# Linear attention plus a gated product on one core: softmax sums carried in the state matrix, one key pass instead of two, and work moved between engines

## Chip, cores, metric

One core of one Trainium2 chip. The metric is device time in microseconds (us) of one execution, as the median of several.

## The reference, cut to what matters

```python
xn = _layernorm(x)                                   # x: 2048 x 512, bf16
# branch A: linear attention, 32 heads of 16
q, k, v = split(xn @ wqkv)                           # per head
pq, pk  = q @ w_phi, k @ w_phi                       # per head, 16 x 16
phi_q   = concat(softmax(pq), softmax(-pq))          # 32 features
phi_k   = concat(softmax(pk), softmax(-pk))
kv, z   = phi_k^T @ v, sum_s phi_k
o       = (phi_q @ kv) / (phi_q . z + 1e-6)
A       = o.reshape(S, D) @ wo
# branch B: gated product
B       = ((xn @ w_gate) * (xn @ w_up)) @ w_down     # F = 1792
return x + A + B
```

## The kernel before

`w_phi` is folded into the q and k weights at the start (transposes and `fold`), so that one product gives `pk` or `pq`. Then come three stages: the key side (layer norm, exp, softmax, `kv`), the query side, and a closing stage with the output products. The gated branch (called GLU below: `gps`, `ups`, `g_sb`, `hT_all`) depends on the layer norm alone. The scheduler, which fixes the order of instructions when the program is built, uses its matmuls to fill TensorE (PE) in the first two stages. Cuts are marked `...`.

```python
def ln_group(ng):                      # 4 tiles of 128 tokens
    ...
    nc.scalar.activation(out=rstd[:], in_=mv[:, 1:2], func=AF.Sqrt, bias=eps_t[:], scale=1.0)
    nc.vector.reciprocal(out=rstd[:], in_=rstd[:])
    ...                                # xn, four transposes for each of 4 column groups
    nc.vector.tensor_copy(out=xnT[...], in_=tp[:])

def a1_tile(p, n, kvps):               # key side; runs for p = 0, 1 and 16 tiles: half the heads each
    pkps = ...                         # 4 matmuls of 512 columns: 256 of pk, 256 of v
    nc.scalar.activation(out=e2k[:, 0, :], in_=pkps[:, 0:2 * P], func=AF.Exp, scale=1.0)
    nc.scalar.activation(out=e2k[:, 1, :], in_=pkps[:, 0:2 * P], func=AF.Exp, scale=-1.0)
    nc.vector.tensor_reduce(out=sums[:], ...); nc.vector.reciprocal(out=rs..., in_=sums[:])
    nc.vector.tensor_tensor(out=phik..., in0=e2k..., in1=rs..., op=ALU.mult)      # 512 wide
    nc.scalar.copy(out=vt[:, :, :, 0:DH], in_=pkps[:, 2 * P:4 * P]...)
    ...                                # 4 matmuls of 136 columns into kvps

# query side, per 256 tokens (m), half (hf) and column group (cql):
    pq = ...                           # 4 matmuls of 256 columns
    nc.scalar.activation(out=ep[:], in_=pq[:], func=AF.Exp, scale=1.0)
    nc.scalar.activation(out=em[:], in_=pq[:], func=AF.Exp, scale=-1.0)
    nc.tensor.matmul(swp[:], lhsT=BO16f, rhs=em[:], start=True, stop=True)   # softmax sums
    nc.tensor.matmul(swm[:], lhsT=BO16f, rhs=ep[:], start=True, stop=True)
    nc.vector.tensor_tensor(out=phip[:], in0=ep[:], in1=swp[:], op=ALU.mult)
    nc.vector.tensor_tensor(out=phim[:], in0=em[:], in1=swm[:], op=ALU.mult)
    for t4 in range(2):                # 256 columns, of which 8 heads x 32
        nc.tensor.matmul(nds[t4][...], lhsT=phip[:, t4 * P:(t4 + 1) * P], rhs=KVZ[:, cq, 0, :], start=True, stop=False)
        nc.tensor.matmul(nds[t4][...], lhsT=phim[:, t4 * P:(t4 + 1) * P], rhs=KVZ[:, cq, 1, :], start=False, stop=True)
    ...                                # on DVE: two small steps, reciprocal, product, copy of oT

# closing stage, per 512 tokens: 14 GLU steps (4 gps + 4 ups matmuls of 512 columns), then
    ...                                # fin: 14 + 4 matmuls of 512 columns, add x, store
```

The sums are used crosswise (`ep` is multiplied by the sum over `em`), because the common factor cancels in the division at the end.

The softmax here doesn't subtract the row's maximum and nothing guards it: scores larger than these inputs give would overflow.

## Time and profile before

| | before |
|---|---|
| median | 271.49 us (271.35 to 272.33, 4 runs) |
| span of the profiled run | 269.6 us |
| granted clock | 1.00 |
| matmuls | 1504, of 566,272 columns |

In the profile, PE is TensorE, PEld its weight loads, DVE VectorE, ACT ScalarE, POOL GpSimd and SP the engine that issues loads and stores. The cuts are the first `kv` product (28.05 us), the end of the last one (104.02) and the first `fin` matmul (173.58). Columns: the stretch, its length, then busy time of PE, PEld, DVE, ACT and POOL, clock, DMA share, GB/s.

```profile
0.00:28.05 28.05, 17.51 (x106) 8.94 (x108) 17.64 (x56) 12.92 (x28) 6.08 (x24) 1.00 0.99 330
28.05:104.02 75.97, 73.74 (x468) 37.35 (x477) 70.47 (x158) 51.67 (x137) 5.04 (x29) 1.00 0.02 7
104.02:173.58 69.56, 68.78 (x493) 44.84 (x498) 61.06 (x219) 29.44 (x75) 0.00 (x0) 1.00 0.00 1
173.58:269.60 96.02, 92.16 (x416) 40.93 (x422) 25.04 (x43) 9.38 (x16) 0.00 (x0) 1.00 0.07 23
```

DVE is 93% busy on the key side (70.47/75.97) and 88% on the query side.

### The profile page before, as it was taken

How to read it: one execution, taken by the hardware profiler on the slowest of the kernel's cores; microseconds unless marked ns; L12 is line 12 of the kernel's file. 1: busy time of each engine (PE TensorE's matmuls, PEld its weight loads, DVE VectorE, ACT ScalarE, POOL GpSimd, SP SyncE). 2: the span in 40 equal slices, each digit the busy share in tenths (PEclk: the TensorE clock that was granted, in tenths of full speed). 3: DMA queues.
4: the chain of work that ended last, by engine and by line, in shares of the span. 5: the costliest groups of instructions: out<-in, count | busy, mean ns of one | idle time of the engine just before them, and what ended most of it. 6: DMA issues, size and time to landing. Idle time of an engine off the chain costs nothing.

```text
span 269.6 us, 4074 instructions
## 1 busy us (share of the span) xinstructions
PE 252.2 (94%) x1476; PEld 132.1 (49%) x1504; DVE 174.2 (65%) x473; ACT 103.4 (38%) x256; POOL 11.1 (4%) x53
## 2 busy tenths in 40 slices
PE   0589998999999999999999999999999999999994
PEld 0344543445555545666666666544444444444441
DVE  4648999886999999988888898821222223333211
ACT  2069396593796663444343434100001001332000
POOL 5300000000000100000000000000000000000000
PEclk9999999999999999999999999999999999999999
DMA  6999400000000000000000000001101000000011
GB/s 247 352 372 348 126 0 1 2 0 0 2 1 4 0 1 2 0 0 4 0 0 2 0 4 1 0 22 39 36 22 41 19 27 32 2 0 0 0 41 39
DMA packets 10996, 12.08 MB, mean 45 GB/s; under 512 B 992, under 2 KB 10464, under 8 KB 10976
## 3 DMA queue, kind: packets, MB, share of 16 engines
q1 hardware_dynamic: 10976, 11.81, 13.0%
q8 instruction: 12, 0.20, 0.3%
q14 instruction: 8, 0.07, 0.1%
HBM read 9.72 MB, written 2.10 MB: 44 GB/s over the span
## 4 chain that ended last, share of the span: by engine, by line
PE 76%; DVE 13%; ACT 7%; issue 2%; DMA 1%; ACTq 0%; DVEq 0%
PE fin L335 18%; PE gps L319 15%; PE ups L324 15%; PE fin L338 5%; PE pq L264 5%; PE pkps L199 4%; DVE phik L211 4%; DVE sums L206 3%; PE nd L283 3%; PE nd L280 3%; PE tp L160 2%; ACT e2k L203 2%; DVE rs L209 2%; DVE hT_all L330 1%; ACT g_sb L329 1%
## 5 line engine op out<-in xcount | busy, mean ns | idle before, releaser
L329 ACT CAST g_sb<-gps 128x512 bf16<-128x512 f32 x56 | 32.9, 588 | 86.0 <-PE gps L319 85.6
L319 PE MATMUL gps<-xnT,wg 128*128 128x512 bf16 x220 | 64.2, 383 | 0.8 <-ACT g_sb L329 0.5
L324 PE MATMUL ups<-xnT,wu 128*128 128x512 bf16 x209 | 61.9, 378 | 0.9 <-DVE hT_all L330 0.4
L330 DVE TENSOR_TENSOR hT_all<-ups,g_sb 128x512 bf16<-128x512 f32 x56 | 38.5, 688 | 23.1 <-PE ups L324 19.8
L335 PE MATMUL fin<-wd,hT_all 128*128 128x512 bf16 x220 | 51.0, 379 | 0.3
L341 DVE TENSOR_TENSOR o_sb<-fin,xall 128x512 bf16<-128x512 f32 x16 | 11.1, 692 | 48.6 <-PE fin L338 45.5
L335 PEld LDWEIGHTS <-hT_all 128*128 128x128 bf16 x224 | 21.8, 98 | 25.7
L199 PE MATMUL pkps<-W1k,xnT 128*128 128x512 bf16 x125 | 33.7, 378 | 0.6 <-ACT vt L216 0.2
L324 PEld LDWEIGHTS <-wu 128*128 128x128 bf16 x224 | 21.4, 97 | 20.7 <-issue 5.2
L319 PEld LDWEIGHTS <-wg 128*128 128x128 bf16 x224 | 21.7, 98 | 18.3 <-issue 1.1
L268 ACT ACTIVATE ep<-pq 128x256 bf16<-128x256 f32 x32 | 12.4, 387 | 33.3 <-PE pq L264 15.8
L264 PE MATMUL pq<-xnT,W1q 128*128 128x256 bf16 x128 | 23.8, 272 | 0.2
L206 DVE TENSOR_REDUCE sums<-e2k 128x32 f32<-128x512 f32 x32 | 21.1, 665 | 2.6 <-ACT e2k L204 2.4
L211 DVE TENSOR_TENSOR phik<-e2k,rs 128x512 bf16<-128x512 f32 x32 | 21.6, 679 | 0.6
L160 PE MATMUL tp<-ident,xn 128*128 128x128 bf16 x64 | 9.1, 239 | 9.8 <-DVE xn L152 7.9
L199 PEld LDWEIGHTS <-xnT 128*128 128x128 bf16 x128 | 11.7, 97 | 11.2 <-issue 1.9
L278 DVE TENSOR_TENSOR phim<-em,swm 128x256 bf16<-128x256 bf16 x32 | 13.3, 415 | 4.8 <-PE swm L274 4.1
L203 ACT ACTIVATE e2k<-pkps 128x256 f32<-128x256 f32 x32 | 13.0, 405 | 8.9 <-DVE phik L211 8.8
L338 PE MATMUL fin<-wo,oT 128*128 128x512 bf16 x62 | 16.2, 379 | 0.1
L264 PEld LDWEIGHTS <-W1q 128*128 128x128 bf16 x128 | 12.3, 97 | 5.3 <-issue 1.6
L280 PE MATMUL nd<-KVZ,phip 128*128 128x256 bf16 x64 | 14.3, 272 | 0.1
L145 DVE BATCH_NORM_STATS2 stats<-xall 128x6 f32<-128x512 bf16 x16 | 10.5, 669 | 5.4 <-DMA xall<-in_A_x_dram 5.4
(60 smaller groups left out, 260.2 us busy)
## 6 DMA issues: line engine op xcount, KB each, us to landing
xall<-in_A_x_dram SPq DMA_DIRECT2D x4, 512.0 KB, 9.7
out_dram<-o_sb SPq DMA_DIRECT2D x16, 128.0 KB, 1.7
wg<-in_B_w_gate_dram SPq DMA_DIRECT2D x2, 896.0 KB, 9.1
wu<-in_B_w_up_dram SPq DMA_DIRECT2D x2, 896.0 KB, 10.5
wd<-in_B_w_down_dram SPq DMA_DIRECT2D x1, 1792.0 KB, 14.3
wqk<-in_A_wqkv_dram SPq DMA_DIRECT2D x1, 1024.0 KB, 6.0
W1k<-in_A_wqkv_dram SPq DMA_DIRECT2D x2, 256.0 KB, 6.6
wo<-in_A_wo_dram SPq DMA_DIRECT2D x1, 512.0 KB, 14.5
```

The source lines that it names most:

```text
L199: nc.tensor.matmul(pkps[:], lhsT=xnT[:, j, n * P:(n + 1) * P], rhs=W1k2[:, j, p, :], start=(j == 0), stop=(j == DC - 1))
L203: nc.scalar.activation(out=e2k[:, 0, :], in_=pkps[:, 0:2 * P], func=AF.Exp, scale=1.0)
L206: nc.vector.tensor_reduce(out=sums[:], in_=e2k[:].rearrange("p s (h f) -> p (s h) f", f=DH), axis=AX.X, op=ALU.add)
L211: nc.vector.tensor_tensor(out=phik[:].rearrange("p (g f) -> p g f", f=DH), in0=e2k[:].rearrange("p s (h f) -> p (s h) f", f=DH), in1=rs[:] ...
L264: nc.tensor.matmul(pq[:], lhsT=W1q[:, j, cq * P:(cq + 1) * P], rhs=xnT[:, j, m * TM:(m + 1) * TM], start=(j == 0), stop=(j == DC - 1))
L280: nc.tensor.matmul(nds[t4][:, cql * 2 * P:(cql + 1) * 2 * P], lhsT=phip[:, t4 * P:(t4 + 1) * P], rhs=KVZ[:, cq, 0, :], start=True, stop=False)
L319: nc.tensor.matmul(gps[:], lhsT=wg[:, c, f * P:(f + 1) * P], rhs=xnT[:, c, T * TT:(T + 1) * TT], start=(c == 0), stop=(c == DC - 1))
L324: nc.tensor.matmul(ups[:], lhsT=wu[:, c, f * P:(f + 1) * P], rhs=xnT[:, c, T * TT:(T + 1) * TT], start=(c == 0), stop=(c == DC - 1))
L329: nc.scalar.copy(out=g_sb[:], in_=gps[:])
L330: nc.vector.tensor_tensor(out=hT_all[:, f, :], in0=ups[:], in1=g_sb[:], op=ALU.mult)
L335: nc.tensor.matmul(fin[:], lhsT=hT_all[:, f, t4 * P:(t4 + 1) * P], rhs=wd[:, f, :], start=(f == 0), stop=False)
L338: nc.tensor.matmul(fin[:], lhsT=oT[:, c, n * P:(n + 1) * P], rhs=wo[:, c, :], start=False, stop=(c == DC - 1))
```

## The change

Its intent is less work on PE and DVE: (1) `E` itself (the exps), not a normalised `phi`, is the stationary operand (the weights, `lhsT`) of the `nd` product. KVZ, the state matrix that holds `kv` and `z` of each head, has one more column per head, of ones, so each product also yields its softmax sum. The two `sw` products go and `nd` shrinks from 256 to 144 columns. DVE combines the two halves. (2) One key pass over 1024 features instead of two over 512. (3) rstd by Ln and Exp, which share a table set with the softmax exp. (4) Copies of `xnT` and `oT` go from DVE to ACT, those of `wT` from ACT to DVE, the last product of the query side to GpSimd. (5) Loads are cut and ordered anew. (6) `pq` works on 512 tokens, with two buffers each for `pq` and `nd`. The diff, cut to its core (renamings, constants, and lines that only move are left out):

```diff
-    dma_x(0)
-    nc.sync.dma_start(out=wqk[:], in_=A_wqkv[:, 0:2 * D].rearrange("(j p) c -> p j c", p=P))
 ...
+    dma_x(0, 1)
+    dma_x(1, 4)
+    dma_cols(wqk, D, A_wqkv, D, 2 * D)           # the key half; the query half comes near the end
+    ...                                          # wphi, wv, first 512 columns of gate and up
+    dma_x(4, 8)
+    ...                                          # rest of gate and up, x, query half, wd, wo
+    nc.scalar.preload_act_table_set("natural_log_exp_and_others")
 ...
-                nc.scalar.activation(out=rstd[:], in_=mv[:, 1:2], func=AF.Sqrt, bias=eps_t[:], scale=1.0)
-                nc.vector.reciprocal(out=rstd[:], in_=rstd[:])
+                nc.scalar.activation(out=rstd[:, ni:ni + 1], in_=mv[:, ni, 1:2], func=AF.Ln, bias=eps_t[:], scale=1.0)
+                nc.scalar.activation(out=rstd[:, ni:ni + 1], in_=rstd[:, ni:ni + 1], func=AF.Exp, scale=-0.5)
 ...
-                nc.vector.tensor_copy(out=xnT[:, c, ng * GT * P:(ng + 1) * GT * P], in_=tp[:])
+                nc.scalar.copy(out=xnT[:, c, ng * TT:(ng + 1) * TT], in_=tp[:])
 ...                                              # a1_tile: all 512 pk columns, then v by a product of its own
+            nc.vector.tensor_reduce(out=sums[:], in_=ev, axis=AX.X, op=ALU.add)
+            nc.vector.reciprocal(out=rs[:].rearrange("p a b -> p (a b)"), in_=sums[:])
+            nc.vector.tensor_tensor(out=phik[:]..., in0=ev, in1=rs[:].to_broadcast((P, 2 * H, DH)), op=ALU.mult)
+            ...                                  # 8 matmuls of 129 columns into kvps
 ...
-                    nc.tensor.matmul(swp[:], lhsT=BO16f, rhs=em[:], start=True, stop=True)
-                    nc.tensor.matmul(swm[:], lhsT=BO16f, rhs=ep[:], start=True, stop=True)
-                    ...                          # phip, phim on DVE
+                    for cl in range(2):
+                        cq = hf * 2 + cl
+                        for s in (1, 0):
+                            mm = nc.tensor.matmul(nd[:, s, cl * HC * J:(cl + 1) * HC * J],
+                                             lhsT=E[:, s, cq, t4 * P:(t4 + 1) * P],
+                                             rhs=KVZ[:, s, cq].rearrange("p h j -> p (h j)"),
+                                             start=True, stop=True)
+                    nc.vector.reciprocal(out=rsm[:], in_=ndv[1][:, :, DH + 1:DH + 2])
+                    nc.vector.tensor_tensor(out=rho[:], in0=ndv[0][:, :, DH + 1:DH + 2], in1=rsm[:], op=ALU.mult)
+                    nc.vector.tensor_tensor(out=tmp[:], in0=ndv[1][:, :, 0:DH + 1], in1=rho[:]..., op=ALU.mult)
+                    nc.vector.tensor_tensor(out=sm[:], in0=ndv[0][:, :, 0:DH + 1], in1=tmp[:], op=ALU.add)
+                    nc.vector.reciprocal(out=rden[:], in_=sm[:, :, DH:DH + 1])
+                    nc.gpsimd.tensor_tensor(out=o_tok[...], in0=sm[:, :, 0:DH], in1=rden[:]..., op=ALU.mult)
```

## The prediction

> **What bounds the kernel now.** I read first the page's engine sums and its slices, then the chain that ended last, then the time line of TensorE alone, then the groups of instructions by shape, then the stretches of 20 us.
>
> ```profile
> PE 252.2 (94%) x1476; PEld 132.1 (49%) x1504; DVE 174.2 (65%) x473; ACT 103.4 (38%) x256; POOL 11.1 (4%) x53
> PE   0589998999999999999999999999999999999994
> DVE  4648999886999999988888898821222223333211
> PEclk9999999999999999999999999999999999999999
> ...
> by line: PE fin L335 17.9%; PE gps L319 15.4%; PE ups L324 14.9%; PE fin L338 5.1%; PE pq L264 5.1%; PE pkps L199 4.3%; DVE phik L211 3.6%; DVE sums L206 3.4%; PE nd L283 3.1%; PE nd L280 2.7%; issue 1.9%; PE tp L160 1.7%; ACT e2k L203 1.5%
> ```
>
> TensorE (PE) is full after the third slice at full clock, and the chain is mostly PE. VectorE (DVE) is nearly as full, but only up to about slice 26. So PE is the bound, with DVE as a second one during attention. "94%" overstates this: matmuls overlap, so their durations don't add. The time line shows the real spacing (start, length of the merged piece; a piece's length includes one pipeline tail):
>
> ```profile
> 177.99 3.02 PE fin L335 x14
> 124.07 0.49 PE L264 MATMUL pq<-xnT,W1q 128*128 128x256 bf16 x3
> 24.13 0.38 PE L160 MATMUL tp<-ident,xn 128*128 128x128 bf16 x4
> ```
>
> 3.02/14 = 0.216 us per 512 columns. The 256-column group: (0.49 - 0.27 for one)/2 = 0.11. The 128-column one: (0.38 - 0.22)/3 = 0.055. So a matmul costs about 0.417 ns per column plus some 2.5 ns, whatever its recorded 378 or 272 ns. By this price the program's 1504 matmuls (864 of 512 columns, 320 of 256, 128 of 136, 192 of 128; 566,272 columns) need 236.0 + 3.8 = 239.7 us. The span is 269.6, so 30 us are lost. Counting the weight loads by line in stretches of 10 us and pricing them the same way puts the loss at: 14 us in the first 20 us, some 7 between 20 and 110 (the key side), 3 between 110 and 180 (the query side), 1 to 2 in the closing stage, and 3.5 after the last matmul.
>
> ```profile
> 0.00:20.00 20.00, 9.56 (x56) 5.11 (x58) 10.30 (x35) 6.56 (x14) 6.08 (x24) 1.00 0.94 323
> 20.00:40.00 20.00, 19.84 (x124) 9.99 (x125) 19.10 (x49) 14.87 (x35) 1.01 (x6) 1.00 0.52 164
> 120.00:140.00 20.00, 19.78 (x145) 13.03 (x145) 17.80 (x67) 8.31 (x22) 0.00 (x0) 1.00 0.00 1
> 180.00:200.00 20.00, 19.89 (x92) 9.09 (x93) 3.46 (x5) 0.00 (x0) 0.00 (x0) 1.00 0.10 34
> ```
>
> (Columns: PE, PE weight loads, DVE, ACT, POOL busy with counts, clock, DMA share, GB/s.) DVE drops from 19.1 to 3.5 of 20 us when attention ends; the GLU and the output product then run on PE alone.
>
> **What the Trainium skill says.** "TensorE: Matmul & The Clock Gate", section Back-to-back issue gap, gives N/2.4 + 2.5 ns; the trace agrees (0.216 for 512 columns). The same section's 131 ns per 512-column matmul in a stream isn't seen here. "ScalarE: Activation LUTs", section Table sets, says that one set holds exp and ln, but exp and sqrt need a switch; What ACT_TABLE_LOAD costs gives 1283 ns. The trace has eight loads of 1283 ns. "VectorE: DVE Perf Modes", section on the TRN2 errata, times an fp32 tensor_tensor as (N+151)/0.96 ns: 691 for 512, and 679 to 692 in this trace; I use it for new sizes. "GPSIMD Engine Reference", section 3.1, counts 2.6 cycles of 1.2 GHz an element with two inputs. The only such case in the trace, 128 elements, took 457 ns.
>
> **The change, part by part.** The order of instructions after it was read from the built program. The GLU's matmuls fill the attention stages in both.
>
> ```profile
> L264 PE MATMUL pq<-xnT,W1q 128*128 128x256 bf16 x128 | 23.8, 272 | 0.2
> L280 PE MATMUL nd<-KVZ,phip 128*128 128x256 bf16 x64 | 14.3, 272 | 0.1
> L274 PE MATMUL swm<-ep,BO 128*128 128x256 bf16 x32 | 8.7, 273 | 0.0
> L278 DVE TENSOR_TENSOR phim<-em,swm 128x256 bf16<-128x256 bf16 x32 | 13.3, 415 | 4.8 <-PE swm L274 4.1
> L209 DVE RECIPROCAL rs<-sums 128x32 f32<-128x32 f32 x32 | 10.8, 343 | 0.3
> L203 ACT ACT_TABLE_LOAD x4 | 5.1, 1283 | 0.1
> ```
>
> (Groups: busy us, mean ns | idle before.)
>
> 1. PE, query side. The softmax sums no longer have their own product: 64 matmuls of 256 columns go (64 x 0.109 = 7.0 us). The sum rides as an extra column in KVZ, and the 128 products of 256 columns become 144 wide (128 x 112 x 0.417 ns = 6.0 us). pq has the same columns in half the instructions (0.2). kv goes from 136 to 129 columns (0.4). All else keeps its columns. Sum: 31,616 columns, 13.2 us, plus 128 fewer instructions, 0.3: PE needs 226.2 us. On a PE-bound kernel all of this is on the path.
>
> 2. DVE, query side. By starts (a DVE instruction starts some 0.08 us before the last one's end): before, per 128 tokens and half, 2 products of 0.33, one of 0.33, small ones 0.36, and 16 copies of oT of 0.33: 48 us in all. After, 32 times (two 16-wide reciprocals of 0.145, one of 0.105, two 272-wide products of 0.35) = 35 us. The final product goes to GpSimd, by the page's rate 0.55 plus some 0.2: 32 x 0.75 = 24 us beside. DVE has slack there: by the new order it needs 52 us where PE needs 66.
>
> 3. DVE, key side. Sixteen tiles of 1024 instead of 32 of 512: reduction and product 1.14 each, reciprocal 0.55 (0.28 at 32, 0.145 at 16) = 2.83, 45 us against 32 x 1.49 = 48. xnT copies (16 x 0.33) go to ACT. From the first to the last kv product PE has 56.8 us of work and DVE 57.4: equal, so neither can be full. In the old kernel DVE was 92 to 95% busy in such a stage. 57.4/0.94 = 61 us, so 4 to 5 us of PE are lost, against 7.
>
> 4. ACT. Seven of eight table loads go (9 us of ACT time, three on the chain in the key stage); rstd takes two ACT steps, Ln and Exp, in place of a square root and a DVE reciprocal. This is part of the loss in point 3. ACT needs some 104 us, no bound.
>
> 5. Start. x's first tile comes alone, and the key half of wqk ahead of the rest. But the first transpose group needs all four tiles, and DVE takes them in turn with two ACT steps each (some 0.7 us from mean to rstd): xn of tile 3 comes near 9 us, where it was 8.8. Then four transpose groups with ACT copies of 0.6 through one buffer end near 13, as now. V products fill that time. I take 12 us lost instead of 14.
>
> 6. Query side and end. pq has two banks, but two exps take 1.2 us a bank against 0.86 for the matmuls: about 1 us of PE in each of four blocks. With the wait for the last transposes I take 5 us lost against 3. The closing stage: 3 instead of 1.5. The tail after the last matmul stays, 3.5.
>
> Sum: 226.2 + 12 + 5 + 5 + 3 + 3.5 = 254.7 us of span, and 271.5 - 269.6 = 1.9 on top: 256.6 us.
>
> **The rivals.** (a) The gain is eaten on the query side: nd has two buffers, each held through a chain of four DVE steps; g has one; oT, exps and g share ACT. Then PE waits more where its filler comes in the wrong order. For: 5 us lost was itself a guess, and the first GpSimd product there is unmeasured. Against: DVE has 13 us of slack and 24 us of GpSimd is spread over 66. If it holds, 262 to 266 us. (b) DVE becomes the bound in the key stage: pk and vp have one buffer each, and in-order DVE holds GLU products and phik in one line. At 85% DVE, 57.4/0.85 = 67.5, 6 us worse than mine: 263. For: work is exactly equal on both; against: the table loads that broke it are gone. (c) It goes better: the start gains 4 us more from the V products and the stages lose as little as the old query stage: 226.2 + 9 + 3.5 + 3 + 2 + 3.5 + 1.9 = 249. (d) Nothing comes of it, because loss grows by the 13 us saved. That needs every stage at its worst.
>
> **Range and chances.** The saved columns are counted, not guessed, and PE's price is the same in every stage seen; only the losses are open, 28.5 us by my sum, 21 to 35 plausible. That gives 250 to 263 us around 256.6. Faster by 2% means under 266.1, which takes 38 us of loss: 0.94 for faster, 0.05 for the same, 0.01 for slower.
>
> **What would show it.** Right: weight loads priced by columns sum to 226 us; no table load after the first; DVE over 90% busy in the key stage and near 80% in the query stage; losses by stage as above. The 1024-wide reduction and product near 1.2 us, the 64-wide reciprocal near 0.6, the GpSimd product near 0.75. Wrong: PE's waits on nd or g grow on the query side (a), PE waits for phik in the key stage (b), or a matmul of 144 columns spaces wider than 0.063 us.

## The result, and the profile after

253.49 us median (252.39 to 254.25, 11 runs) against 272.15 for the kernel before in the same rounds (271.29 to 273.75, 16 runs). The ratio is 0.9315, 95% interval 0.9295 to 0.9334. A ratio here is the mean time of one kernel's fast runs over that of the other's of the same rounds, so not quite the ratio of the medians. The gain is 0.0685 x 272.15 = 18.6 us.

The page of the changed kernel, engine sums and slices:

```profile
PE 237.0 (94%) x1350; PEld 116.7 (46%) x1376; DVE 150.7 (60%) x343; ACT 103.2 (41%) x209; POOL 25.2 (10%) x57
PE   0599999999999999999999999999999999999994
DVE  3367899999966992795997969911212213343221
```

PE's share is 94% as before: that number would have told nobody that the span got 17.1 us shorter. (The profiled run of the changed kernel took 254.16 us, 0.7 above its median, so spans show a little less of the gain than the ratio does.) DVE fell from 174 to 151 us. The stages, cut at the same events, in the windows view:

```profile
0.00:31.82 31.82, 22.46 (x128) 11.17 (x131) 18.93 (x44) 17.80 (x45) 5.30 (x25) 1.00 0.93 306
31.82:93.22 61.40, 59.94 (x391) 31.16 (x398) 56.33 (x81) 36.85 (x77) 0.00 (x0) 1.00 0.00 1
93.22:166.06 72.84, 71.96 (x464) 37.62 (x472) 56.15 (x192) 41.64 (x78) 19.90 (x32) 1.00 0.01 1
166.06:252.50 86.44, 82.67 (x371) 36.71 (x376) 19.28 (x28) 6.86 (x12) 0.00 (x0) 1.00 0.07 25
```

Stage lengths can't be compared directly, because the scheduler puts different amounts of GLU filler into each. The prediction's price (columns x 0.417 ns + 2.5 ns a matmul) gives a common measure: add up the prices of all matmuls that stand before an event in the built program's PE order, and subtract that from the time of the event in the trace. This is the time that PE has lost so far; from one event to the next it is the loss of that stage.

| loss in us | start, to first kv | key side, to last kv | query side, to first fin | closing, to last matmul | after it | priced work | span |
|---|---|---|---|---|---|---|---|
| before | 14.6 | 6.4 | 3.2 | 2.3 | 3.4 | 239.7 | 269.6 |
| after | 14.2 | 4.1 | 2.9 | 1.7 | 3.4 | 226.2 | 252.5 |
| predicted after | 12 | 5 | 5 | 3 | 3.5 | 226.2 | 254.7 |

Of the 17.1 us of span, 13.5 are priced work, 2.3 the key side, and 1.3 the rest. On the key side PE waited less for `phik`, before and after in the waits view (what waited, for what: us in total, times, longest):

```profile
PEld L221 <- DVE phik L211: 8.9, 26, 0.9
PEld L203 <- DVE phik L198: 2.3, 9, 0.5
```

In the chain of waits the `sw` products are gone. The groups that were priced ahead, by shape (busy us, mean ns | idle before):

```profile
L257 PE MATMUL nd<-KVZ,E 128*128 128x144 bf16 x128 | 13.8, 226 | 0.1
L194 DVE TENSOR_REDUCE sums<-e 128x64 f32<-128x1024 f32 x16 | 19.2, 1201 | 0.5 <-ACT e L185 0.4
L196 DVE RECIPROCAL rs<-sums 128x64 f32<-128x64 f32 x16 | 8.6, 542 | 0.0
L270 DVE TENSOR_TENSOR sm<-nd,tmp 128x272 f32<-128x272 f32 x32 | 13.7, 428 | 0.8
L273 POOL TENSOR_TENSOR o_tok<-sm,rden 128x256 bf16<-128x256 f32 x32 | 19.9, 622 | 135.6 <-DVE rden L272 114.8
L91 ACT ACT_TABLE_LOAD x1 | 1.3, 1283 | 0.8 <-PEq L328 0.8
```

One table load is left of eight, and the durations are near those expected (1.2, 0.6, 0.44 and 0.75 us). One thing in the trace the prediction had not seen: PE's time line in the first 17 us.

```profile
14.13 0.63 PE L188 MATMUL vp<-wv,xnT 128*128 128x512 bf16 x1
14.56 0.63 PE L290 MATMUL g<-xnT,wg 128*128 128x512 bf16 x1
14.98 0.63 PE L295 MATMUL u<-xnT,wu 128*128 128x512 bf16 x1
...
16.22 0.38 PE L290 MATMUL g<-xnT,wg 128*128 128x512 bf16 x1
16.44 0.38 PE L295 MATMUL u<-xnT,wu 128*128 128x512 bf16 x1
```

Up to about 16 us a 512-column matmul starts 0.43 us after the last one and lasts 0.63; then 0.22 and 0.38. PE runs at half rate, though the clock column says 1.00. The kernel before does the same (0.63 us each up to 14.7).

### The profile page after: what moved, and what is told of

Same layout as the page of the kernel before. It is cut to its first block, busy times and chain, and to the rows that moved or that the text cites. A ratio compares the mean times of both kernels' runs of the same rounds, so it can differ in the third digit from the quotient of the medians.

```text
span 252.5 us, 3600 instructions
## 1 busy us (share of the span) xinstructions
PE 237.0 (94%) x1350; PEld 116.7 (46%) x1376; DVE 150.7 (60%) x343; ACT 103.2 (41%) x209; POOL 25.2 (10%) x57
## 4 chain that ended last, share of the span: by engine, by line
PE 77%; DVE 14%; ACT 4%; issue 2%; DMA 1%; POOL 0%; SPq 0%; POOLq 0%; DVEq 0%; ACTq 0%
PE fin L306 19%; PE u L295 17%; PE g L290 16%; PE fin L309 5%; PE pq L244 5%; DVE sums L194 5%; PE nd L257 3%; DVE phik L198 3%; PE vp L188 3%; PE tp L152 2%; PE pk L181 2%; DVE hT L301 2%; PE kv L203 2%; DVE rs L196 1%; DMA xall<-in_A_x_dram 1%
## 5 line engine op out<-in xcount | busy, mean ns | idle before, releaser
L300 ACT CAST g_sb<-g 128x512 bf16<-128x512 f32 x56 | 32.9, 588 | 87.2 <-PE g L290 81.3
L290 PE MATMUL g<-xnT,wg 128*128 128x512 bf16 x221 | 63.4, 382 | 0.5 <-ACT g_sb L300 0.3
L295 PE MATMUL u<-xnT,wu 128*128 128x512 bf16 x216 | 62.2, 382 | 0.7 <-DVE hT L301 0.2
L306 PE MATMUL fin<-wd,hT 128*128 128x512 bf16 x220 | 50.9, 379 | 0.3
L301 DVE TENSOR_TENSOR hT<-u,g_sb 128x512 bf16<-128x512 f32 x56 | 38.5, 687 | 21.2 <-PE u L295 19.9
L306 PEld LDWEIGHTS <-hT 128*128 128x128 bf16 x224 | 21.9, 98 | 26.4
L273 POOL TENSOR_TENSOR o_tok<-sm,rden 128x256 bf16<-128x256 f32 x32 | 19.9, 622 | 135.6 <-DVE rden L272 114.8
L194 DVE TENSOR_REDUCE sums<-e 128x64 f32<-128x1024 f32 x16 | 19.2, 1201 | 0.5 <-ACT e L185 0.4
L198 DVE TENSOR_TENSOR phik<-e,rs 128x1024 bf16<-128x1024 f32 x16 | 19.4, 1211 | 0.0
L188 PE MATMUL vp<-wv,xnT 128*128 128x512 bf16 x62 | 18.9, 394 | 0.3
## 6 DMA issues: line engine op xcount, KB each, us to landing
wd<-in_B_w_down_dram SPq DMA_DIRECT2D x1, 1792.0 KB, 13.5
```

The costliest lines, as they stand in the source:

```text
L188: nc.tensor.matmul(vp[:], lhsT=xnT[:, j, n * P:(n + 1) * P], rhs=wv[:, j, :], start=(j == 0), stop=(j == DC - 1))
L194: nc.vector.tensor_reduce(out=sums[:], in_=ev, axis=AX.X, op=ALU.add)
L198: nc.vector.tensor_tensor(out=phik[:].rearrange("p s (h f) -> p (s h) f", f=DH), in0=ev, in1=rs[:].to_broadcast((P, 2 * H, DH)), op=ALU.mult)
L273: nc.gpsimd.tensor_tensor(out=o_tok[:, hf * 256:(hf + 1) * 256].rearrange("p (h d) -> p h d", d=DH), in0=sm[:, :, 0:DH], in1=rden[:].to_br ...
L290: nc.tensor.matmul(gps[:], lhsT=wg[:, c, f * P:(f + 1) * P], rhs=xnT[:, c, T * TT:(T + 1) * TT], start=(c == 0), stop=(c == DC - 1))
L295: nc.tensor.matmul(ups[:], lhsT=wu[:, c, f * P:(f + 1) * P], rhs=xnT[:, c, T * TT:(T + 1) * TT], start=(c == 0), stop=(c == DC - 1))
```

## The experiments

All outputs are right. In what follows, the "cost" of an experiment on the changed kernel is the difference of its ratio from the 0.9315 of the changed kernel, times 272.15 us, and carries about 1 us of uncertainty (1.6 us in e8). The stage losses come from the one profiled run of each. The start's loss alone moves by up to 1 us where nothing there was changed (13.2 in e1, 13.4 in e10, 14.2 in the changed kernel), so smaller differences in it are not read. The scheduler orders each variant anew.

### e1: the nd products 256 columns wide again

```diff
-    KVZ = wpool.tile([P, 2, CQ, HC, J], BF16, name="KVZ")
+    KVZf = wpool.tile([P, 8 * CW + 112], BF16, name="KVZ")      # CW = HC * J = 144; KVZ is a view of it
-    nc.tensor.matmul(nd[:, s, cl * HC * J:(cl + 1) * HC * J], ..., rhs=KVZ[:, s, cq]...)
+    nc.tensor.matmul(nd[:, s, cl * CW:cl * CW + 256], ..., rhs=KVZf[:, (s * CQ + cq) * CW:(s * CQ + cq) * CW + 256])
```

> The changed kernel with the 128 nd products streamed 256 columns wide again (the 112 extra columns are overwritten or unread). Theory (every PE column on the query side is on the path): 128 x 112 x 0.417 ns = 6.0 us more, 259.5 us, ratio to before 0.954. Rival (the query side waits on DVE and buffers, so columns there are hidden): under 1.5 us more, 255 or less.

259.08 us, ratio 0.9539 (0.9512 to 0.9566): 6.1 us for 6.0 expected. The columns cost their full price.

### e2: e1, and the 64 removed sum products as well

```diff
+                    for s in range(2):
+                        nc.tensor.matmul(nd[:, s, 0:256], lhsT=BO16[:]..., rhs=E[:, s, hf * 2, 0:256], start=True, stop=True)
                     for cl in range(2):
```

> As e1, and also the 64 products of 256 columns that the change removed are issued again, into a PSUM region that the next product overwrites; nothing waits for them. Theory: 6.0 + 64 x 0.109 = 13.0 us more than the changed kernel, 266.5 us, ratio 0.979. Rival: under 3 us more, 256.5 or less.

266.94 us, ratio 0.9828 (0.9800 to 0.9857): 14.0 us. The profiled span is 265.5, 13.0 above the changed kernel's. Nothing waits for these columns and no DVE work came with them, so they cost PE time alone. About three quarters of the gain are thereby shown to be PE columns. With 565,376 columns e2 has nearly as many as the kernel before (566,272), and is still 4.7 us faster than it (0.0172 x 272.15): that is what all the other parts of the change are worth together.

### e3: the last product of the query side on DVE

```diff
-                    nc.gpsimd.tensor_tensor(out=o_tok[...], ...)
+                    nc.vector.tensor_tensor(out=o_tok[...], ...)
```

> The changed kernel with the last product of each half on DVE instead of GpSimd: 32 x some 0.33 us = 10.6 us more of DVE work on the query side. Theory (PE bound there, DVE has 13 us of slack): 0 to 1.5 us more, at most 255. Rival (DVE bounds the query side, and moving work to GpSimd was a main part of the gain): 5 us or more, 258.5 up.

254.28 us, ratio 0.9359 (0.9337 to 0.9382): 1.2 us. DVE's busy time rose from 151 to 161 us, and the scheduler answered by placing more GLU filler on the query side. The loss there rose from 2.9 to 4.1, and PE's waits for `sm`, the last DVE step that holds an `nd` buffer, from 2.1 to 4.6 us. GpSimd is worth about 1 us here, not a main part.

### e4: copies of xnT on DVE

```diff
-                nc.scalar.copy(out=xnT[...], in_=tp[:])
+                nc.vector.tensor_copy(out=xnT[...], in_=tp[:])
```

> The changed kernel with the 16 copies of xnT on DVE instead of ACT, as before the change: 5.3 us more of DVE work, four of the copies at the start (where a DVE copy is 0.17 us shorter than ACT's), twelve in the key stage. Theory (DVE and PE bound the key stage together): 1.5 to 4 us more, 255 to 257.5. Rival (PE alone bounds it, its losses come from one-buffer waits): between -1 and +0.5 us.

254.71 us, ratio 0.9377 (0.9358 to 0.9396): 1.7 us, inside the theory's range. But the key side's loss in its trace is 4.7, only 0.6 above; the rest is spread. It agrees with DVE as a second bound of the key side, weakly.

### e5 and e6: the table loads, put back and taken away

e5, on the changed kernel:

```diff
-    nc.scalar.preload_act_table_set("natural_log_exp_and_others")
-    nc.scalar.activation(out=rstd..., in_=mv..., func=AF.Ln, bias=eps_t[:], scale=1.0)
-    nc.scalar.activation(out=rstd..., in_=rstd..., func=AF.Exp, scale=-0.5)
+    nc.scalar.activation(out=rstd..., in_=mv..., func=AF.Sqrt, bias=eps_t[:], scale=1.0)
+    nc.vector.reciprocal(out=rstd..., in_=rstd...)
```

> The changed kernel with rstd by Sqrt on ACT and a reciprocal on DVE again, and no preloaded set. The built program then has 18 table loads (the kernel before had 8): 23 us of ACT time, 22 more than now. Theory (a load in the key stage holds exp, then phik, then kv, and PE and DVE are both full there): 0.3 to 0.6 us a load, 5 to 10 us more, 258.5 to 263.5. Rival (ACT has slack, loads are hidden): under 1.5 us more.

261.13 us, ratio 0.9589 (0.9561 to 0.9616): 7.5 us for 17 more loads, net of the other steps of the swap. The key side's loss is 10.4 us in place of 4.1. Its stretch in the windows view:

```profile
31.96:96.68 64.72, 58.55 (x389) 30.01 (x390) 56.87 (x82) 53.70 (x87) 0.00 (x0) 1.00 0.00 1
```

ACT (the fourth engine) is now 53.7 of 64.7 us busy, where it was 36.9 of 61.4.

e6 is the same edit the other way round, on the kernel before: Ln, Exp and the preload in place of Sqrt and reciprocal, all else as it was.

> The kernel before with only rstd by Ln and Exp and the preloaded set: one table load in place of 8. Theory (loads cost 0.3 to 0.6 us each in the key stage): 2 to 4 us faster than before, ratio 0.985 to 0.993. Rival (hidden): within 0.5 us, ratio 0.998 to 1.002.

271.27 us (16 runs), ratio to before 0.9969 (0.9954 to 0.9984): 0.8 us. The key side's loss fell from 6.4 to 5.4. So the seven loads that the change removed had cost 0.1 us each, again net of the other steps, a third of the least that I had expected. In e5 a load costs 0.44. One reading is that loads were rarer in the kernel before and had room beside other ACT work, but e5 also has another order of instructions, so the difference isn't settled. The rstd step by itself is a small part of the gain.

### e7 and e9: the loads

e7 has the old order and sizes of the loads:

```diff
-    dma_x(0, 1); dma_x(1, 4); dma_cols(wqk, D, A_wqkv, D, 2 * D); ...
+    dma_x(0, 4); dma_cols(wqk, 0, A_wqkv, 0, 2 * D); ...      # gate and up in halves of 896
```

> The changed kernel with the old order and sizes of the loads (x in chunks of four tiles, both halves of wqk at once, gate and up in halves of 896). Theory (the new order bought next to nothing, since work priced by columns at the first kv product lay 14.2 us behind, against 14.6): within 1 us of the changed kernel, 252.5 to 254.5. Rival (it bought 2 us or more that something else ate): 255.5 or more.

256.23 us, ratio 0.9405 (0.9376 to 0.9434): 2.4 us. My theory that the new order bought next to nothing fell. About 1.5 us of the loss sit on the key side (5.6 against 4.1). The start shows 14.6 against 14.2, but e1, e2 and e3, whose start was not changed, have 13.2 to 13.6, so some 1 us can lie there too. Its key stretch:

```profile
30.23:90.13 59.90, 57.73 (x393) 30.12 (x392) 57.52 (x86) 37.51 (x81) 0.00 (x0) 1.00 0.01 1
```

DVE is 96% busy there (57.52/59.90), where it was 92%, and at the first `kv` product it had done 15.65 us of work instead of 18.93, because the layer norm of the second four tiles came later. So I supposed that the new order let DVE do this layer norm while it idles. e9 tests that with one moved line:

```diff
     dma_cols(wu, 0, B_w_up, 0, 512)
-    dma_x(4, 8)
     dma_cols(wg, 512, B_w_gate, 512, F)
     dma_cols(wu, 512, B_w_up, 512, F)
+    dma_x(4, 8)
     dma_x(8, 12)
```

> The changed kernel with one load moved: x's tiles 4 to 7 come behind the rest of gate and up instead of ahead of them; all else keeps its place. e7 cost 2.4 us, and its DVE had done 15.7 us of work at the first kv product where the changed kernel's had done 18.9. Theory (what the new load order bought is the layer norm of tiles 4 to 7 done while DVE idles at the start, instead of in the key stage, which DVE bounds): 1.5 to 3 us more than the changed kernel, most of it in the key stage. Rival (it was the first tile of x and the split of wqk at the start): within 0.7 us.

253.56 us (5 rounds), ratio 0.9333 (0.9299 to 0.9368): 0.5 us, within noise, and a key side loss of 3.9. The edit did what it was meant to do: at the first `kv` product DVE had done 15.19 us of work. So that supposition fell too. Which of the other differences in e7 (the lone first tile, the halves of wqk, the first 512 columns of gate and up) carries the 2.4 us stays open.

### e10: the key side in pieces of 512

```diff
-            nc.vector.tensor_reduce(out=sums[:], in_=ev, ...); nc.vector.reciprocal(...); nc.vector.tensor_tensor(out=phik[:], ...)
+            for s in range(2):                   # the same three, 512 wide, for each half
+                nc.vector.tensor_reduce(out=sums[:, hs], in_=ev[:, hs, :], axis=AX.X, op=ALU.add)
+                ...
```

> The changed kernel with sums, reciprocal and phik of each tile in two parts of 512 instead of one of 1024 (the kernel before worked in 512s). 48 more DVE instructions; by start-to-start costs 16 x 0.15 = 2.4 us more DVE work, all in the key stage. Theory (DVE bounds that stage): 1 to 3 us more. Rival (shorter pieces release kv and exp earlier, and PE's waits shrink): -1 to +0.5 us.

253.29 us, ratio 0.9316 (0.9290 to 0.9342): nothing. Its key stretch:

```profile
29.67:90.13 60.46, 59.10 (x379) 30.60 (x385) 58.71 (x126) 35.81 (x76) 0.00 (x0) 1.00 0.01 2
```

DVE is 97% busy and the loss is 3.9 us, as with 92%. So in the changed kernel DVE had room on the key side, and wider DVE instructions are no source of the gain. What the other 4 us of loss there are made of isn't settled.

### e8 and e11: PE warmed up ahead

```diff
+        wm = consts.tile([P, 256], BF16, name="wm")
+        nc.vector.memset(wm[:], 1.0)
+        wps_ = ps_gu.tile([P, TT], F32, name="u")
+        for _ in range(32):                      # 24 in e11
+            nc.tensor.matmul(wps_[:, 0:256], lhsT=wm[:, 0:P], rhs=wm[:], start=True, stop=True)
         ln_group(0)
```

> The changed kernel with 32 dummy matmuls of 256 columns on a constant tile ahead of everything on PE. In both traces a 512-column matmul takes 0.63 us and spaces at 0.43 until about 16 us, then 0.38 and 0.216. Theory (PE starts at half rate and needs some us of work to reach full rate, and the start is partly bound by that): the first real matmuls space at 0.216, and 1 to 3 us are gained, 250.5 to 252.5. Rival (the start is bound by the row-by-row layer norm and by loads alone): within 0.5 us.

> The changed kernel with 24 dummy matmuls ahead instead of 32, to end nearer the first transpose (the 32 ended 1.1 us after the first normalised tile was there). Theory (half rate costs at the start): first kv product 2 us earlier than in the changed kernel, 250 to 252 us, ratio 0.918 to 0.926. Rival (given back in the key stage or the closing): 0.929 to 0.934.

e8: 253.02 us, but its four runs lie between 251.87 and 255.38; ratio 0.9302 (0.9246 to 0.9358), not to be told from the changed kernel's 0.9315. e11: 254.29 us, ratio 0.9345 (0.9322 to 0.9368), so no gain. The profiles tell the two apart. The dummies of e8 and one of the transposes after them, then those of e11, on PE's time line:

```profile
1.28 5.76 PE L211 MATMUL u<-wm 128*128 128x256 bf16 x32 [1.28 <-DVE wm L208]
...
8.83 0.23 PE L152 MATMUL tp<-ident,xn 128*128 128x128 bf16 x1 [0.87 <-DVE xn L146]
```

```profile
1.28 4.84 PE L211 MATMUL u<-wm 128*128 128x256 bf16 x24 [1.28 <-DVE wm L208]
...
6.68 0.23 PE L152 MATMUL tp<-ident,xn 128*128 128x128 bf16 x1 [0.51 <-DVE xn L146]
7.97 0.23 PE L152 MATMUL tp<-ident,xn 128*128 128x128 bf16 x1 [1.06 <-DVE xn L146]
9.07 0.29 PE L152 MATMUL tp<-ident,xn 128*128 128x128 bf16 x1 [0.87 <-DVE xn L146]
```

At half rate 256 columns take 0.213 us, at full rate 0.109. For 24 to fit in 4.84 us, and 32 in 5.76, some 20 each must have gone at half rate, so PE reached full rate after about 4.3 us of unbroken work. In e12, below, the same 24 took 5.30 us, so all went at half rate: the moment differs from run to run. In e8's profiled run the full rate stayed: its matmuls after 9.7 us last 0.38 us, and the first `kv` product starts at 29.54 us instead of 31.82. In e11 PE fell back to half rate (from 10.4 us on 512 columns last 0.63 us again), as the clock column shows (e11, windows view):

```profile
5.00:10.00 5.00, 1.92 (x12) 1.05 (x11) 3.38 (x10) 2.08 (x7) 1.62 (x4) 0.89 1.01 309
10.00:15.00 5.00, 4.97 (x21) 2.56 (x21) 0.69 (x1) 1.75 (x3) 0.00 (x0) 0.50 1.07 377
15.00:20.00 5.00, 4.64 (x32) 2.66 (x32) 3.93 (x12) 2.73 (x8) 0.00 (x0) 0.93 1.05 384
```

The Trainium skill, "TensorE: Matmul & The Clock Gate", Part 1, says that PE starts at half rate, is released by some 3.4 us of sustained work, and is held back again after an idle window, with the moment varying from run to run. The runs agree on the half rate and roughly on the time. Why e11 fell back is not shown: the same transposes followed the dummies in e8's profiled run, with gaps nearly as long (up to 0.87 us), and it did not fall back. PE was busy for 1.92 us between 5 and 10 us in e11 and for 2.88 in e8, so too little work is a likely reason.

e8's runs differ because the clock fell back in some of them: the granted clock was 1.000 in the run of 251.87 us, 0.993 in those of 252.99 and 253.06, and 0.986 in that of 255.38. By these shares PE was held at half rate again for some 3.5 us in two runs and 7 us in one (an estimate: twice the missing share, times the span). In e11 all four runs have 0.984 to 0.986. So PE fell back for a time in seven of eight runs, and what the warm-up is worth when it holds rests on one run.

### e12: e11, and half of phik on GpSimd

```diff
-            nc.vector.tensor_tensor(out=phik[:], in0=ev, in1=rs..., op=ALU.mult)
+            for s, eng in ((1, nc.gpsimd), (0, nc.vector)):
+                eng.tensor_tensor(out=phik[:, s, :]..., in0=ev[:, hs, :], in1=rs[:, hs, :]..., op=ALU.mult)
```

> As e11, and half of each phik product (512 of 1024) on GpSimd, which is idle in the key stage: 16 x 0.53 us = 8.5 us less DVE work there, 16 products of some 1.2 us on GpSimd. Theory (DVE bounds the key stage): 1 to 3 us below e11, key-stage loss from 4 to about 2 us. Rival (DVE and GpSimd slow each other when both read two SBUF operands, or the longer way to kv makes PE wait): no gain or a loss of up to 3 us.

262.15 us, ratio 0.9641 (0.9616 to 0.9666): 8.1 us worse than e11 (0.0296 x 272.15). The rival holds, at more than the 3 us that it had allowed. The key side's loss is 11.2 us. The view of the tile `phik` (durations in ns as minimum, median and maximum):

```profile
L200 POOL TENSOR_TENSOR phik<-e,rs x16: 1056/1265/1579, 28.7 to 86.7; 128x512 bf16<-128x512 f32 x16
L200 DVE TENSOR_TENSOR phik<-e,rs x16: 677/694/1542, 29.6 to 86.6; 128x512 bf16<-128x512 f32 x16
```

PE and its weight loads waited 19.7 us for `phik` in all, 18.0 of it for GpSimd's half. DVE's half mostly takes 694 ns, but up to 1542. The Trainium skill, "GPSIMD Engine Reference", section 1, says that GpSimd's SBUF ports are shared with VectorE, in contention with DVE instructions that have two SBUF inputs; both halves here have two. The doubled maximum agrees with that. By the waits, though, most of the cost is the longer way from `rs` through GpSimd to `kv`.

No version that ran is clearly faster than the changed kernel.

## Why the prediction was right

It said 256.6 us, 250 to 263, and 253.49 came. None of its signs of being wrong showed. PE's waits for `phik` fell (8.9 to 2.3 us). Its waits on the query side for what DVE, ACT and GpSimd make fell too, from 6.2 to 4.9 us in all. The product after four `nd` products starts 0.25 us after the first of them (106.38 to 106.63 us on the time line), so 144 columns space at 0.0625 us, not over 0.063. DVE was 92% busy on the key side and 77% on the query side, for "over 90%" and "near 80%". Step by step:

1. **PE, query side: right.** 13.5 us of priced work less, and e2 measured 14.0 for 13.0 of it put back. "On a PE-bound kernel all of this is on the path" held to within the error.
2. **DVE, query side: right in kind.** DVE was 56 of 73 us busy there, no bound; e3 gave 10 us of work back to it for 1.2 us of time. The GpSimd product took 0.62 us for 0.75.
3. **DVE, key side: the size right, the reason not fully.** The loss was 4.1 for "4 to 5", and the durations agreed. But e10 shows that DVE could do some 2 us more there for nothing, so "neither can be full" because both have equal work isn't the whole cause.
4. **ACT and table loads: over-weighted.** They were named as part of the drop on the key side; e6 gives 0.8 us for all seven.
5. **Start: wrong in size.** 12 us lost against 14.2. The working priced the start at full rate, and "PE's price is the same in every stage seen" fails there: up to 16 us PE goes at half rate, in both kernels, so the V products that were to fill the start cost double. The gain of the new load order (2.4 us in e7) was placed at the start; e7's trace shows about 1.5 us of it on the key side. (Rival (c) also has a slip: 12 less 4 is 8, not 9.)
6. **Query side and closing: too dark.** 5 and 3 us against 2.9 and 1.7. I had added a stall of 1 us in each of four blocks for the two-bank `pq`; in the trace PE waits 1.5 us in all for `E`. The query side lost hardly less than before (3.2), so little that none of rival (a) is seen.

The losses sum to 26.3 us against 28.5 expected: the start was 2.2 us worse, key side, query side and closing together 4.3 better. That these errors cancel in part, so that the median lies only 3.1 us under the prediction, is luck; the 13.5 us of columns are not. The rest of the 3.1 us is that the profiled run lies 0.7 us above the median, and that its time beside the span is 1.7 us (254.16 - 252.5) instead of 1.9.

## What to carry to other kernels

When PE's gaps are filled by independent matmuls, count columns: a change that removes columns is worth their full price, and one that relieves another engine by 10 us may be worth 1. Don't judge by PE's busy share, which was 94% before and after; price the matmuls in program order and read the loss at a few events. Before moving elementwise work to GpSimd, look at what waits for its result: on the query side, off the path, it gained about 1 us; ahead of `kv` it cost 8 us.

## What the Trainium skill lacked or had wrong

- "TensorE: Matmul & The Clock Gate", section Back-to-back issue gap: its 131 ns for a 512-column matmul in a sustained stream isn't reached; 14 of them took 3.02 us, 216 ns each, and e1 and e2 confirm that price.
- The same page, section Why this matters for your kernels, asks for no PE gap over about 3 us. In e11 no gap after the dummies was over 1.1 us, yet PE fell back to half rate (clock 0.50); e8's profiled run, with gaps up to 0.87 us, did not. So a limit on single gaps is not enough; the work between them may count, which is not shown.
- The same page warns that clock events can be unreliable; the runs show one case: until the first rise the clock column says 1.00 while 512 columns take 0.43 us.
- "VectorE: DVE Perf Modes" names the reciprocal's repeat of 8 but gives no time: means of 241 to 252 ns at 16 elements, 321 (e10) to 343 (the kernel before) at 32, and 542 at 64.
- "GPSIMD Engine Reference", section 3.1, times a product of two inputs at one size, 2048 elements; here a product of 256 took 622 ns, and one of 512 took 1265 beside DVE.
